# Attention followed by a gated convolution on one core: the order in which one queue issues stores and loads

## The chip, the core and the metric

The kernel runs on one core of a Trainium2 chip. A core has a matrix engine (TensorE, PE in the profile; its weight loads stand apart as PEld), a vector engine (VectorE, DVE), an engine for activation functions and copies (ScalarE, ACT), a general engine (GpSimd, POOL) and a sync engine (SyncE, SP) that computes nothing and here issues every DMA. The engines run at the same time. Each works off its own list of instructions in order and waits at an instruction until what it needs is there. The metric is the time of one execution in microseconds (us) on the device; lower is better.

## What is computed

Two steps, batch 4, 768 positions, 8 heads of 64. First an attention in which each query sees the keys nearer than 16 positions and, beside them, 24 summaries of the whole sequence, one for each block of 32 positions (the maximum of its keys, the mean of its values). Then a gated causal convolution over the 512 joined channels, and an output matrix.

```python
k_sum = k.reshape(B, H, nb, block, D).max(axis=3)          # block 32, nb 24
v_sum = v.reshape(B, H, nb, block, D).mean(axis=3)
scores_l = where(abs(i - j) < 16, scale * q @ k.T, -1e9)
scores_s = scale * q @ k_sum.T + log(block)
a = softmax(concat([scores_l, scores_s]))
x = a @ concat([v, v_sum])                                 # (4, 768, 512)
gate_pre = sum(conv_w[t] * shifted(x, t) for t in range(5))
out = (sigmoid(gate_pre) * (x @ w_val)) @ w_out            # (4, 768, 512) f32
```

## The kernel before

The rows are cut into 12 groups g (batch b and third of the sequence, 256 rows each), and the attention of a group into two units u = 2g and 2g + 1 (four heads each), 24 units in all. A group's result is two tiles `out` of 128 rows by 512 columns, named (g, 0) and (g, 1).

Nothing schedules this program at run time or compile time. One string, `ORDER`, holds some 1,400 tokens such as `S.13.0`; a loop at the end of the kernel function calls for each token the function of that name with those numbers. Each function emits its instructions, so the string sets for every engine the order of its list. A framework adds the waits that the data need. The tokens that matter here:

- `q.g` (line 270), `k.b.pr`, `v.g.e` (line 285), `n.b.pr` (the transposed values `vT`, line 281): loads from HBM, all on SP. `q` has two buffers, `qbd0` and `qbd1`; group g uses number g mod 2.
- `f.g.e` (line 368): an SP copy of the block means into the v tile of group g, inside SBUF. Part e = 0 or 1 serves the even or the odd query tiles of 64 rows.
- `S.u.r` (line 438), PE: scores. `N` (454), DVE: mask and row minimum. `E` (468), ACT: exponentials. `M` (481), POOL: division by the row sum. `T` (490), PE: transposes into `pt`. `C` (494), ACT: copies `pt` to `pts`, which frees the memory for a later `S`. `X` (508), PE: times v.
- `tr.b.pr` (326), POOL (a few DVE): block sums from `vT`.
- `V` (558), `O` (587), PE: the products with `w_val` and `w_out`. `oe.g.si` (597), ACT: evicts an out tile into the SBUF tile `ob`, halved on the way. `st.g.si` (606), SP: stores it.

`op_X` goes through its query tiles in the order 0, 2, 1, 3, so its first half reads part e = 0 of the v tile and its second half part e = 1. The tile `ob` has two buffers for the 24 out tiles; an eviction waits until the store of the tile two before it has left its buffer:

```python
ob = wt(("ob", g, si), [P, DM], "ob")            # a pool with bufs=2
nc.scalar.activation(ob, po, AF.Copy, scale=0.5) # op_oe
...
nc.sync.dma_start(out[b, r0 : r0 + P, w], ob[:, w])  # op_st
```

SP too is in order: a store that waits for its eviction holds every load behind it.

Of the kernel before, what the change touches and what calls it, by code (L numbers as in the profile page):

```python
# [81 lines left out]
G.6 S.12.0 N.12.1 N.12.0 tr.2.1 H.8 I.8.1 N.13.2 N.12.3 N.13.0 E.12.3 k.3.1 f.5.0 N.12.2 N.13.1
M.11.1 A.8.0 A.8.1 A.8.2 O.2.0 oe.2.0 X.9 E.13.0 F.9 I.9.0 st.2.0 v.6.0 E.12.2 I.9.1 A.8.3 A.8.4 H.9
E.12.0 T.10 C.10.0 E.12.1 A.9.0 A.9.1 C.10.1 M.11.0 E.13.1 E.13.2 V.3.0 gf.3.0 A.8.5 A.8.6 A.9.2
A.8.7 V.3.1 gf.3.1 VS.2 vs.2 A.9.3 R.13 A.9.4 A.9.5 R.12 A.9.6 A.9.7 T.11 C.11.0 L.8 L.9 C.11.1 X.10
X.11 gh.3.0 S.14.1 S.15.1 S.15.0 S.14.0 N.14.3 N.14.2 F.10 N.15.1 H.10 h.5 gl.3.0 M.13.0 G.8 H.11
V.4.1 G.9 I.10.1 F.11 I.10.0 I.11.0 I.11.1 gh.3.1 N.14.0 L.10 A.10.0 E.14.3 N.14.1 k.3.3 ks.3.3
# [3 lines left out]
gh.4.0 O.3.0 C.12.0 E.15.0 C.13.0 C.13.1 oe.3.0 M.14.0 gl.4.1 L.11 gl.4.0 S.16.1 f.6.1 S.17.1 S.16.0
S.17.0 E.15.3 G.11 E.15.1 G.10 f.6.0 n.3.0 v.7.0 st.3.1 X.13 I.13.0 ks.3.0 F.13 I.13.1 X.12 N.17.1
V.5.0 H.13 H.12 I.12.1 F.12 kc.3.0 N.16.2 R.15 N.16.3 N.17.0 A.13.0 N.16.0 A.13.1 I.12.0 V.5.1
M.14.1 v.8.0 v.7.1 f.7.1 v.8.1 A.12.0 N.17.2 st.3.0 f.8.0 f.7.0 L.13 E.17.0 gf.5.0 N.17.3 A.12.1
# [9 lines left out]
I.16.1 F.16 gf.7.1 H.16 A.16.0 X.17 S.21.1 I.17.1 gh.7.1 F.17 S.21.0 A.16.1 N.21.1 N.21.0 S.20.1
L.16 M.19.0 I.17.0 S.20.0 A.17.0 E.21.0 H.17 A.17.1 N.20.2 N.21.3 N.20.1 N.21.2 N.20.0 V.7.0 gf.7.0
N.20.3 st.5.0 v.9.0 v.9.1 M.18.0 E.21.3 O.6.1 st.5.1 E.20.2 E.20.0 A.16.2 A.16.3 A.17.2 A.17.3
A.16.4 oe.6.1 VS.3 vs.3 f.9.0 gh.7.0 gl.7.1 A.17.4 A.17.5 A.16.5 A.16.6 T.18 A.17.6 A.17.7 C.18.1
M.19.1 T.19 C.19.1 E.20.3 C.19.0 C.18.0 L.17 V.8.0 E.21.1 G.17 E.21.2 E.20.1 A.16.7 R.20 O.6.0
oe.6.0 f.9.1 X.19 q.11 v.10.1 G.16 H.19 F.19 X.18 I.19.0 v.11.0 S.23.1 h.9 R.21 M.21.1 M.21.0 F.18
# [8 lines left out]
C.22.1 A.20.2 A.20.3 A.20.4 C.22.0 V.10.1 gf.10.1 A.20.5 A.20.6 O.8.0 oe.8.0 A.20.7 G.20 X.22 F.22
X.23 I.22.0 h.11 A.22.0 H.22 L.22 A.22.1 I.22.1 V.10.0 gf.10.0 F.23 H.23 L.23 O.9.1 I.23.0 I.23.1
V.11.0 oe.9.1 A.22.2 st.9.1 A.23.0 A.23.1 gh.10.0 A.23.2 A.23.3 A.23.4 A.23.5 A.23.6 A.23.7 gh.10.1  # L120
gl.10.0 G.23 V.11.1 gf.11.1 A.22.3 st.8.0 O.9.0 oe.9.0 st.9.0 A.22.4 A.22.5 gl.10.1 O.10.1 A.22.6
A.22.7 G.22 gf.11.0 gh.11.0 gh.11.1 O.10.0 gl.11.1 oe.10.1 oe.10.0 st.10.0 gl.11.0 O.11.0 oe.11.0
st.10.1 O.11.1 oe.11.1 st.11.0 st.11.1
"""


# [572 lines left out]
```

## Time and profile before

| | us |
|---|---|
| median of 3 runs | 232.5 (232.01 to 234.11) |
| the profiled execution | 233.51 |
| its span (first to last instruction) | 231.4 |
| PE busy | 218.8 (95% of the span) |
| ACT busy | 187.1 (81%) |
| DVE busy | 171.0 (74%) |
| POOL busy | 150.9 (65%) |
| SP's DMA queue, share of 16 DMA engines | 57.1% |

The profile is of one execution. Busy time is the time in which an engine runs an instruction; issuing a DMA and waiting do not count. On a timeline, a bracket at the end of a row says how long the engine was idle before it, and what ended that. Rows of SP are the times at which it issues a DMA, not those at which the data move. One row can stand for several instructions in a row (x4), and lines are those of the listing above.

### The profile page before, as it was taken

The numbers are of one execution on the slowest core, as the hardware profiler recorded it, in microseconds if no ns is written. First come the engines' busy times: TensorE is split into PE (matmuls) and PEld (weight loads), VectorE is DVE, ScalarE is ACT, GpSimd is POOL, SyncE is SP. The second block draws the span as 40 slices with busy tenths as digits, with TensorE's granted clock in tenths as the row PEclk, the third lists the DMA queues.
The fourth block names the chain that finished last, engine by engine and source line by source line (L and its number), as shares of the span: only waits on it lengthen the run. The fifth ranks groups of instructions, "written<-read, shape, count | busy, mean of one in ns | idle before, by whom it ended". The sixth has DMA issues, their size and how long they took to land.

```text
span 231.4 us, 7645 instructions
## 1 busy us (share of the span) xinstructions
PE 218.8 (95%) x2828; PEld 185.3 (80%) x2828; DVE 171.0 (74%) x699; ACT 187.1 (81%) x614; POOL 150.9 (65%) x207
## 2 busy tenths in 40 slices
...
GB/s 235 341 389 369 408 410 281 406 364 179 318 353 217 283 174 219 305 82 290 284 29 184 183 118 140 180 177 3 130 145 319 89 48 19 46 0 93 45 91 91
DMA packets 17052, 46.50 MB, mean 201 GB/s; under 512 B 2136, under 2 KB 3160, under 8 KB 17016
## 3 DMA queue, kind: packets, MB, share of 16 engines
q1 hardware_dynamic: 17016, 46.02, 57.1%
...
## 4 chain that ended last, share of the span: by engine, by line
PE 66%; DMA 18%; ACT 10%; DVE 4%; issue 1%; SPq 1%; ACTq 0%
PE out L587 23%; PE val L558 23%; DMA k<-in_kT_dram 7%; PE s L438 7%; PE x L508 7%; DMA raw_wo<-in_wo_dram 5%; ACT p L468 4%; PE pt L490 4%; DMA out_dram<-ob 3%; DMA qbd<-in_qT_dram 3%; DVE g L538 2%; PE pw L332 1%; PE vb L342 1%; ACT g L533 1%; DVE sn L454 1%
## 5 line engine op out<-in xcount | busy, mean ns | idle before, releaser
L538 DVE SCALAR_TENSOR_TENSOR g<-xf,cwt,g 128x256 f32<-128x256 f32 x192 | 87.5, 484 | 14.3 <-ACT g L533 8.6
L468 ACT ACTIVATE p<-sn,nm 128x120 f32<-128x120 f32 x192 | 74.0, 396 | 10.5 <-DVE nm L454 10.3
L481 POOL TENSOR_TENSOR p<-p,ri 128x480 f32<-128x480 f32 x48 | 46.8, 991 | 23.9 <-DVE ri L476 21.5
L558 PE MATMUL val<-xh,wv 128*128 128x256 f32 x352 | 49.6, 283 | 0.0
L454 DVE CUSTOM_DVE_ANT_0 sn<-s,mask 128x120 f32<-128x120 f32 x192 | 42.7, 276 | 6.0 <-PE s L438 4.5
L558 PEld LDWEIGHTS val<-xh,wv 128*128 128x128 f32 x352 | 44.5, 188 | 1.4 <-issue 0.3
L587 PE MATMUL out<-wo,gh 128*128 128x512 f32 x176 | 45.1, 398 | 0.0
L572 POOL TENSOR_TENSOR gl<-gf,gh 128x512 fp32r<-128x512 f32 x22 | 28.3, 1294 | 18.1 <-ACT gh L567 18.0
L468 ACT ACTIVATION_READ_ACCUMULATOR p<-sn,nm 128x1 f32 x192 | 38.3, 200 | 0.0
L587 PEld LDWEIGHTS out<-wo,gh 128*128 128x128 f32 x176 | 31.7, 188 | 6.9 <-ACT gt L544 0.2
L524 POOL TENSOR_TENSOR xl<-xf,xh 128x512 fp32r<-128x512 f32 x22 | 28.2, 1292 | 7.9 <-ACT xh L516 7.8
L438 PE MATMUL s<-k,qbd 64*64 64x120 f32 x768 | 26.3, 280 | 6.9 <-POOL k L315 2.7
L438 PEld LDWEIGHTS s<-k,qbd 64*64 64x64 f32 x768 | 21.0, 139 | 11.1 <-POOL k L315 3.9
L326 POOL TENSOR_TENSOR vT<-vT 128x384 f32<-128x384 f32 (+3 forms) x48 | 27.3, 570 | 2.8
L597 ACT ACTIVATE ob<-out 128x512 f32<-128x512 f32 x23 | 13.7, 597 | 18.1 <-PE out L587 14.5
L558 PE MATMUL val<-xl,wv 128*128 128x256 f32 x176 | 27.7, 279 | 0.0
L494 ACT COPY pts<-pt 120x512 f32<-120x512 f32 x48 | 26.3, 589 | 1.5 <-PE pt L490 1.4
L508 PEld LDWEIGHTS x<-pts,v 120*64 120x64 f32 x768 | 23.6, 138 | 3.7 <-ACT pts L494 1.1
L508 PE MATMUL x<-pts,v 120*64 120x64 f32 x768 | 25.4, 224 | 0.4 <-DVE low_wo L394 0.4
L563 DVE SCALAR_TENSOR_TENSOR gf<-gt,val 128x512 f32<-128x512 f32 x24 | 16.4, 685 | 11.9 <-PE val L558 5.7
L587 PE MATMUL out<-wo,gl 128*128 128x512 f32 x88 | 24.1, 395 | 0.0
L558 PEld LDWEIGHTS val<-xl,wv 128*128 128x128 f32 x176 | 23.7, 188 | 0.0
...
## 6 DMA issues: line engine op xcount, KB each, us to landing
...
```

What stands on the lines that cost most here:

```text
L326: nc.gpsimd.tensor_tensor(dst, src[:, :, :n], src[:, :, n : 2 * n], ALU.add)
L438: nc.tensor.matmul(sp[64 * e : 64 * e + 64, h, c * KW : c * KW + KW], qbd[g % NQB][64 * h : 64 * h + 64, pr, i * QT : i * QT + QT], ktile( ...
L454: nc.vector.tensor_tensor_reduce(sn[:, n, :], tiles["s", u][:, h, c * KW : c * KW + KW], mask[:, mv, :], -1.0 / math.sqrt(D), 3.0e38, ALU.add,
L468: nc.scalar.activation(p[:, n, :], tiles["sn", u][:, n, :], AF.Exp, bias=tiles["nm", u][:, n : n + 1], scale=-1.0, accum_out=rs[:, u % NRS ...
L481: nc.gpsimd.tensor_tensor(p[:, w], p[:, w], ri[:, w].unsqueeze(2).broadcast_to([P, TPU, KW]), ALU.mult)
L494: nc.scalar.copy(pts[:, :, QT * e : QT * e + QT], tiles["pt", u][:KW, e])
L508: nc.tensor.matmul(dst, w, src, start=True, stop=True)
L524: nc.gpsimd.tensor_tensor(xl[:, prs(u), :], xf(g)[:, prs(u), HALO:], tiles["xh", g][:, prs(u), :].bitcast(F32), ALU.subtract,)
L538: nc.vector.scalar_tensor_tensor(gt, xf(u // NHP)[:, pr, o : o + SG], cwt[:, pr, o : o + 1], gt, ALU.mult, ALU.add)
L558: nc.tensor.matmul(val[:, r], w, x, start=(n == 0), stop=(n == len(terms) - 1))
L572: nc.gpsimd.tensor_tensor(gl[:, cos, :], tiles["gf", g, cp], tiles["gh", g][:, cos, :].bitcast(F32), ALU.subtract)
L587: nc.tensor.matmul(po, x, w, start=(n == 0), stop=(n == len(terms) - 1))
```

## The change

Only the string `ORDER` changes: 13 of the 24 stores come earlier in SP's list, ahead of loads, copies or another store. The tokens of the loads and of all computing keep their order among themselves. Two pieces of the diff:

```diff
-E.7.2 woc.2 F.4 H.4 A.3.5 R.7 k.2.1 q.5 v.3.0 A.3.6 A.3.7 N.9.3 I.4.0 A.4.0 N.9.2 G.3 gf.1.1 F.5
+E.7.2 woc.2 F.4 H.4 A.3.5 R.7 st.0.0 k.2.1 q.5 v.3.0 A.3.6 A.3.7 N.9.3 I.4.0 A.4.0 N.9.2 G.3 gf.1.1
...
+kc.2.1 F.7 ks.2.0 N.11.0 X.6 I.7.1 H.7 M.9.0 st.1.1 q.7 M.9.1 I.7.0 gl.2.0 A.7.0 N.11.2 A.7.1 A.7.2
...
-n.2.3 A.7.4 v.5.1 v.5.0 st.1.1 A.6.0 A.6.1 A.7.5 H.6 A.7.6 E.11.2 E.11.3 oe.1.0 st.1.0 gl.2.1 h.4
```

The instructions on PE, DVE, ACT and POOL stand in the same order before and after. SP's list changes. In the names below the digits behind the first word are those of the token (`v_4` is the v tile of group 4, `ob_1_1` the evicted tile (1,1)), and the last number only counts. SP's list before, from the copy `f.4.0` on:

```order
L368 DMA v_4_1239<-vs_1_1186 24x2x512
L270 DMA qbd1_70<-in_qT_dram 128x1024
L270 DMA qbd0_69<-in_qT_dram 128x1024
L368 DMA v_4_1239<-vs_1_1186 24x2x512
L281 DMA vT_2_2_1440<-in_vT_dram 128x768
L281 DMA vT_2_3_1449<-in_vT_dram 128x768
L285 DMA v_5_1452<-in_vw_dram 128x1024 x2
L606 DMA out_0_dram<-ob_1_1_1372 128x512
L606 DMA out_0_dram<-ob_1_0_1465 128x512
L368 DMA v_5_1452<-vs_1_1186 24x2x512
L606 DMA out_0_dram<-ob_2_1_1541 128x512
```

and in the same place after the change:

```order
L368 DMA v_4_1240<-vs_1_1187 24x2x512
L606 DMA out_0_dram<-ob_1_1_1372 128x512
L270 DMA qbd1_70<-in_qT_dram 128x1024
L270 DMA qbd0_69<-in_qT_dram 128x1024
L368 DMA v_4_1240<-vs_1_1187 24x2x512
L281 DMA vT_2_2_1441<-in_vT_dram 128x768
L281 DMA vT_2_3_1450<-in_vT_dram 128x768
L285 DMA v_5_1453<-in_vw_dram 128x1024 x2
L606 DMA out_0_dram<-ob_1_0_1465 128x512
L606 DMA out_0_dram<-ob_2_1_1541 128x512
L368 DMA v_5_1453<-vs_1_1187 24x2x512
```

The store of tile (1,1) stood behind the two halves of the v load of group 5. Now it stands ahead of both q loads (groups 7 and 6), of the copy `f.4.1`, of two vT loads and of the v loads. The store of tile (2,1) moves ahead of a copy for group 5.

The second place is on SP, around the stores of group 3. Before:

```order
L273 DMA k_3_2_2050<-in_kT_dram 128x968
L368 DMA v_6_1695<-vs_2_1797 24x2x512 x2
L281 DMA vT_3_0_2177<-in_vT_dram 128x768
L285 DMA v_7_2179<-in_vw_dram 128x1024
L606 DMA out_0_dram<-ob_3_1_2035 128x512
L285 DMA v_8_2301<-in_vw_dram 128x1024
L285 DMA v_7_2179<-in_vw_dram 128x1024
L368 DMA v_7_2179<-vs_2_1797 24x2x512
L285 DMA v_8_2301<-in_vw_dram 128x1024
L606 DMA out_0_dram<-ob_3_0_2127 128x512
```

and after:

```order
L273 DMA k_3_2_2050<-in_kT_dram 128x968
L606 DMA out_0_dram<-ob_3_1_2035 128x512
L368 DMA v_6_1695<-vs_2_1797 24x2x512 x2
L281 DMA vT_3_0_2178<-in_vT_dram 128x768
L606 DMA out_0_dram<-ob_3_0_2127 128x512
L285 DMA v_7_2181<-in_vw_dram 128x1024
L285 DMA v_8_2302<-in_vw_dram 128x1024
L285 DMA v_7_2181<-in_vw_dram 128x1024
L368 DMA v_7_2181<-vs_2_1797 24x2x512
L285 DMA v_8_2302<-in_vw_dram 128x1024
```

The store of (3,1) now stands ahead of the two copies `f.6.1` and `f.6.0`, the load of `vT_3_0` and the first v load of group 7; the store of (3,0), the last of the rows before, is now ahead of the v loads of groups 7 and 8. Of the other moves, `st.0.0` goes ahead of a k load, `q.5` and two v loads; `st.4.0` and `st.5.0` each ahead of a vT load, `st.5.1` ahead of the v loads of group 9, `st.6.1` ahead of the copies and the q load behind them, `st.6.0` ahead of the v loads of groups 10 and 11, `st.7.1` and `st.7.0` each ahead of one load or copy, and `st.10.1` ahead of `st.10.0`.

## Rows read from the trace of the kernel before

**Rows 1.** Busy time, calls and rates by stretch: us, engines, PE clock, DMA share, GB/s.
```profile
0.00:52.00 52.00, 44.34 (x573) 31.01 (x577) 41.22 (x195) 43.23 (x157) 31.55 (x58) 1.00 0.97 356
52.00:86.00 34.00, 33.73 (x520) 29.40 (x517) 32.83 (x131) 32.28 (x113) 31.48 (x46) 1.00 0.77 259
86.00:228.00 142.00, 140.69 (x1740) 124.92 (x1740) 96.56 (x374) 111.40 (x347) 87.89 (x104) 1.00 0.40 133
```

**Rows 2.** Timeline of PE (start us, us, engine, line, operation, tiles; idle in brackets).
```profile
84.01 1.15 PE L508 MATMUL x<-pts,v 120*64 120x64 f32 x32
85.09 0.64 PE L438 MATMUL s<-k,qbd 64*64 64x120 f32 x16
87.05 1.46 PE L438 MATMUL s<-k,qbd 64*64 64x120 f32 x48 [1.32 <-ACT pts L494]
```

**Rows 3.** Timeline of ACT around the eviction that waits.
```profile
75.62 0.57 ACT L597 ACTIVATE ob<-out 128x512 f32<-128x512 f32 x1
...
82.88 1.55 ACT L494 COPY pts<-pt 120x512 f32<-120x512 f32 x3
85.93 0.60 ACT L597 ACTIVATE ob<-out 128x512 f32<-128x512 f32 x1 [1.50 <-DMA out_dram<-ob]
86.42 0.58 ACT L494 COPY pts<-pt 120x512 f32<-120x512 f32 x1
```

**Rows 4.** Chain of waits: start us, us, what.
```profile
28.57 11.05 DMA raw_wo<-in_wo_dram
...
77.90 7.94 DMA out_dram<-ob
```

**Rows 5.** Timeline of SP, its DMA issues from 67 to 83 us.
```profile
67.69 2.79 SPq L368 DMA_DIRECT2D v<-vs  x3
71.42 0.81 SPq L270 DMA_DIRECT2D qbd<-in_qT_dram  x2
72.29 0.82 SPq L368 DMA_DIRECT2D v<-vs  x1
73.15 2.67 SPq L281 DMA_DIRECT2D vT<-in_vT_dram  x2
77.00 0.81 SPq L285 DMA_DIRECT2D v<-in_vw_dram  x2
77.90 0.38 SPq L606 DMA_DIRECT2D out_dram<-ob  x1
```

**Rows 6.** The stretch 72.0 to 75.6 us, columns as in the first group.
```profile
72.00:75.60 3.60, 3.60 (x36) 2.81 (x38) 3.46 (x14) 3.60 (x14) 3.29 (x7) 1.00 0.89 312
```

**Rows 7.** Timeline of SP and PE, 108 to 164 us.
```profile
108.94 1.65 SPq L368 DMA_DIRECT2D v<-vs  x2
...
113.17 0.34 SPq L606 DMA_DIRECT2D out_dram<-ob  x1
...
118.29 2.08 PE L508 MATMUL x<-pts,v 120*64 120x64 f32 x64
...
163.13 1.70 SPq L368 DMA_DIRECT2D v<-vs  x2
```

**Rows 8.** The stretch 163.1 to 166.1 us, columns as in the first group.
```profile
163.10:166.10 3.00, 3.00 (x38) 2.93 (x34) 2.89 (x7) 3.00 (x10) 0.00 (x0) 1.00 0.32 69
```

**Rows 9.** Timeline of POOL and PE, 83 to 100 us.
```profile
83.04 2.51 POOL L326 TENSOR_TENSOR vT<-vT 128x384 f32<-128x384 f32 x4
...
94.79 1.94 POOL L481 TENSOR_TENSOR p<-p,ri 128x480 f32<-128x480 f32 x2
...
99.42 0.69 PE L490 MATMUL pt<-ident,p 64*120 64x64 f32 x16
```

**Rows 10.** Timeline of SP, ACT and PE, 55 to 63 us.
```profile
55.08 0.51 SPq L273 DMA_DIRECT2D k<-in_kT_dram  x1
57.26 0.33 SPq L270 DMA_DIRECT2D qbd<-in_qT_dram  x1
...
55.64 0.58 ACT L597 ACTIVATE ob<-out 128x512 f32<-128x512 f32 x1
...
62.56 1.05 PE L438 MATMUL s<-k,qbd 64*64 64x120 f32 x32
```

More of the change, by code (lines that the diff above doesn't have):

```diff
@@ L70 @@
 M.6.0 E.7.0 N.7.2 N.7.3 S.9.1 G.2 gf.1.0 A.3.4 N.9.0 f.2.0 f.2.1 X.5 X.4 V.1.1 E.7.1 E.7.3 N.9.1
-E.7.2 woc.2 F.4 H.4 A.3.5 R.7 k.2.1 q.5 v.3.0 A.3.6 A.3.7 N.9.3 I.4.0 A.4.0 N.9.2 G.3 gf.1.1 F.5
-tr.1.0 S.10.1 H.5 S.10.0 N.10.1 gh.1.0 A.4.1 L.4 gh.1.1 I.5.0 I.4.1 N.10.2 N.10.3 E.10.3 I.5.1
+E.7.2 woc.2 F.4 H.4 A.3.5 R.7 st.0.0 k.2.1 q.5 v.3.0 A.3.6 A.3.7 N.9.3 I.4.0 A.4.0 N.9.2 G.3 gf.1.1
+F.5 tr.1.0 S.10.1 H.5 S.10.0 N.10.1 gh.1.0 A.4.1 L.4 gh.1.1 I.5.0 I.4.1 N.10.2 N.10.3 E.10.3 I.5.1
 N.10.0 ks.2.1 A.4.2 A.5.0 L.5 gl.1.0 A.4.3 M.7.0 M.8.0 T.6 gl.1.1 M.7.1 A.5.1 A.4.4 A.4.5 A.5.2
@@ L74 @@
 A.4.6 A.4.7 VS.1 vs.1 V.2.0 V.2.1 A.5.3 v.4.1 S.11.0 E.9.0 E.9.2 E.10.0 C.6.0 E.10.2 C.6.1 G.4 A.5.4
-gf.2.0 E.9.3 E.10.1 gh.2.0 st.0.0 v.3.1 ks.2.2 R.10 A.5.5 A.5.6 k.2.0 v.4.0 A.5.7 S.11.1 N.11.3
-E.9.1 R.9 h.3 T.7 wob.1 wob.2 C.7.0 n.2.0 tr.2.0 O.1.1 C.7.1 f.3.1 f.3.0 X.7 f.4.0 G.5 gf.2.1 oe.1.1
-N.11.1 kc.2.1 F.7 ks.2.0 N.11.0 X.6 I.7.1 H.7 M.9.0 q.7 M.9.1 I.7.0 gl.2.0 A.7.0 N.11.2 A.7.1 A.7.2
+gf.2.0 E.9.3 E.10.1 gh.2.0 v.3.1 ks.2.2 R.10 A.5.5 A.5.6 k.2.0 v.4.0 A.5.7 S.11.1 N.11.3 E.9.1 R.9
@@ L78 @@
+h.3 T.7 wob.1 wob.2 C.7.0 n.2.0 tr.2.0 O.1.1 C.7.1 f.3.1 f.3.0 X.7 f.4.0 G.5 gf.2.1 oe.1.1 N.11.1
+kc.2.1 F.7 ks.2.0 N.11.0 X.6 I.7.1 H.7 M.9.0 st.1.1 q.7 M.9.1 I.7.0 gl.2.0 A.7.0 N.11.2 A.7.1 A.7.2
 O.1.0 I.6.0 q.6 F.6 E.11.0 I.6.1 gh.2.1 kc.2.2 M.8.1 f.4.1 n.2.2 ks.2.3 kc.2.0 M.10.1 kc.2.3 A.7.3
-n.2.3 A.7.4 v.5.1 v.5.0 st.1.1 A.6.0 A.6.1 A.7.5 H.6 A.7.6 E.11.2 E.11.3 oe.1.0 st.1.0 gl.2.1 h.4
-tr.2.2 A.6.2 A.6.3 M.10.0 L.6 T.9 T.8 C.8.1 L.7 C.8.0 tr.2.3 C.9.1 O.2.1 oe.2.1 C.9.0 E.11.1 A.7.7
-G.7 X.8 F.8 A.6.4 S.13.0 f.5.1 S.12.1 A.6.5 A.6.6 R.11 st.2.1 n.2.1 I.8.0 S.13.1 N.13.3 E.13.3 A.6.7
@@ L82 @@
[L82 to L87, printed above, removed]
@@ L88 @@
-A.11.0 gf.4.1 gl.3.1 V.4.0 N.15.3 gh.4.1 E.14.0 E.14.2 A.10.1 O.3.1 q.8 E.14.1 N.15.2 E.15.2 n.3.3
-q.9 oe.3.1 M.12.0 v.6.1 k.3.0 N.15.0 A.11.1 A.10.2 A.10.3 A.11.2 gf.4.0 A.11.3 k.3.2 A.10.4 A.11.4
+n.2.3 A.7.4 v.5.1 v.5.0 A.6.0 A.6.1 A.7.5 H.6 A.7.6 E.11.2 E.11.3 oe.1.0 st.1.0 gl.2.1 h.4 tr.2.2
+A.6.2 A.6.3 M.10.0 L.6 T.9 T.8 C.8.1 L.7 C.8.0 tr.2.3 C.9.1 O.2.1 oe.2.1 C.9.0 E.11.1 A.7.7 G.7 X.8
+F.8 A.6.4 S.13.0 st.2.1 f.5.1 S.12.1 A.6.5 A.6.6 R.11 n.2.1 I.8.0 S.13.1 N.13.3 E.13.3 A.6.7 G.6
+S.12.0 N.12.1 N.12.0 tr.2.1 H.8 I.8.1 N.13.2 N.12.3 N.13.0 E.12.3 k.3.1 f.5.0 N.12.2 N.13.1 M.11.1
@@ new lines @@
+A.8.0 A.8.1 A.8.2 O.2.0 oe.2.0 X.9 E.13.0 F.9 I.9.0 st.2.0 v.6.0 E.12.2 I.9.1 A.8.3 A.8.4 H.9 E.12.0
+T.10 C.10.0 E.12.1 A.9.0 A.9.1 C.10.1 M.11.0 E.13.1 E.13.2 V.3.0 gf.3.0 A.8.5 A.8.6 A.9.2 A.8.7
+V.3.1 gf.3.1 VS.2 vs.2 A.9.3 R.13 A.9.4 A.9.5 R.12 A.9.6 A.9.7 T.11 C.11.0 L.8 L.9 C.11.1 X.10 X.11
+gh.3.0 S.14.1 S.15.1 S.15.0 S.14.0 N.14.3 N.14.2 F.10 N.15.1 H.10 h.5 gl.3.0 M.13.0 G.8 H.11 V.4.1
+G.9 I.10.1 F.11 I.10.0 I.11.0 I.11.1 gh.3.1 N.14.0 L.10 A.10.0 E.14.3 N.14.1 k.3.3 ks.3.3 A.11.0
+gf.4.1 gl.3.1 V.4.0 N.15.3 gh.4.1 E.14.0 E.14.2 A.10.1 O.3.1 q.8 E.14.1 N.15.2 E.15.2 n.3.3 q.9
@@ L90 @@
+oe.3.1 M.12.0 v.6.1 k.3.0 N.15.0 A.11.1 A.10.2 A.10.3 A.11.2 gf.4.0 A.11.3 k.3.2 A.10.4 A.11.4
 A.11.5 A.11.6 R.14 h.6 M.12.1 kc.3.3 M.13.1 ks.3.2 T.12 C.12.1 A.11.7 T.13 A.10.5 A.10.6 A.10.7
[L91 to L94, printed above, removed]
+gh.4.0 O.3.0 C.12.0 E.15.0 C.13.0 C.13.1 oe.3.0 M.14.0 gl.4.1 L.11 gl.4.0 S.16.1 st.3.1 f.6.1 S.17.1
@@ L95 @@
+S.16.0 S.17.0 E.15.3 G.11 E.15.1 G.10 f.6.0 n.3.0 st.3.0 v.7.0 X.13 I.13.0 ks.3.0 F.13 I.13.1 X.12
+N.17.1 V.5.0 H.13 H.12 I.12.1 F.12 kc.3.0 N.16.2 R.15 N.16.3 N.17.0 A.13.0 N.16.0 A.13.1 I.12.0
+V.5.1 M.14.1 v.8.0 v.7.1 f.7.1 v.8.1 A.12.0 N.17.2 f.8.0 f.7.0 L.13 E.17.0 gf.5.0 N.17.3 A.12.1
 A.12.2 N.16.1 E.16.3 E.16.2 E.16.0 E.16.1 gh.5.0 M.15.0 L.12 M.15.1 A.12.3 A.13.2 A.13.3 A.13.4
@@ L99 @@
 S.18.0 I.14.1 S.18.1 N.18.2 R.16 M.16.1 N.18.3 E.18.3 H.14 O.4.0 oe.4.0 A.14.0 A.15.0 N.19.3 N.19.2
-L.14 E.19.3 L.15 A.15.1 A.15.2 M.16.0 N.19.1 A.14.1 A.14.2 n.3.2 A.14.3 V.6.0 gf.6.0 N.18.0 st.4.0
+L.14 E.19.3 L.15 A.15.1 A.15.2 M.16.0 N.19.1 A.14.1 A.14.2 st.4.0 n.3.2 A.14.3 V.6.0 gf.6.0 N.18.0
 f.8.1 q.10 E.19.0 N.18.1 gh.6.1 E.19.2 M.17.0 M.17.1 A.14.4 A.15.3 A.14.5 A.15.4 A.14.6 A.15.5
-A.15.6 E.18.1 E.18.2 gh.6.0 E.18.0 R.18 O.5.0 oe.5.0 A.14.7 gl.6.0 tr.3.2 M.18.1 n.3.1 tr.3.1 gl.6.1
-V.7.1 T.16 C.16.0 E.19.1 T.17 C.17.0 A.15.7 C.17.1 G.14 C.16.1 G.15 O.5.1 oe.5.1 R.19 X.16 I.16.0
@@ L104 @@
[L104 to L109, printed above, removed]
@@ L110 @@
-H.18 I.19.1 gf.8.0 M.20.0 v.10.0 A.19.0 S.22.1 I.18.0 A.18.0 I.18.1 S.22.0 A.18.1 S.23.0 st.6.1
+A.15.6 E.18.1 E.18.2 gh.6.0 E.18.0 R.18 O.5.0 oe.5.0 A.14.7 gl.6.0 tr.3.2 M.18.1 st.5.0 n.3.1 tr.3.1
+gl.6.1 V.7.1 T.16 C.16.0 E.19.1 T.17 C.17.0 A.15.7 C.17.1 G.14 C.16.1 G.15 O.5.1 oe.5.1 R.19 X.16
+I.16.0 I.16.1 F.16 gf.7.1 H.16 A.16.0 X.17 S.21.1 I.17.1 gh.7.1 F.17 S.21.0 A.16.1 N.21.1 N.21.0
+S.20.1 L.16 M.19.0 I.17.0 S.20.0 A.17.0 E.21.0 H.17 A.17.1 N.20.2 N.21.3 N.20.1 N.21.2 N.20.0 V.7.0
+gf.7.0 N.20.3 st.5.1 v.9.0 v.9.1 M.18.0 E.21.3 O.6.1 E.20.2 E.20.0 A.16.2 A.16.3 A.17.2 A.17.3
@@ L111 @@
+A.16.4 oe.6.1 VS.3 vs.3 st.6.1 f.9.0 gh.7.0 gl.7.1 A.17.4 A.17.5 A.16.5 A.16.6 T.18 A.17.6 A.17.7
+C.18.1 M.19.1 T.19 C.19.1 E.20.3 C.19.0 C.18.0 L.17 V.8.0 E.21.1 G.17 E.21.2 E.20.1 A.16.7 R.20
+O.6.0 oe.6.0 f.9.1 X.19 q.11 st.6.0 v.10.1 G.16 H.19 F.19 X.18 I.19.0 v.11.0 S.23.1 h.9 R.21 M.21.1
+M.21.0 F.18 H.18 I.19.1 gf.8.0 M.20.0 v.10.0 A.19.0 S.22.1 I.18.0 A.18.0 I.18.1 S.22.0 A.18.1 S.23.0
 M.20.1 h.10 N.23.0 N.22.0 N.23.2 A.19.1 gl.7.0 L.18 N.22.1 E.22.0 V.8.1 N.22.2 gf.8.1 f.10.1 L.19
 N.23.1 N.22.3 gh.8.0 gl.8.0 A.19.2 A.18.2 N.23.3 O.7.1 E.22.1 gh.8.1 gl.8.1 V.9.1 E.22.3 E.23.2
-oe.7.1 E.22.2 E.23.0 st.6.0 A.18.3 A.18.4 R.22 M.22.1 A.18.5 A.19.3 A.19.4 A.19.5 O.7.0 oe.7.0
```

19 lines of the change are left out of this document (10 added, 9 removed).

## The prediction

> **What bounds the kernel now.** I read first how busy each engine is in three stretches of the span [rows 1]. From 86 to 228 us TensorE (PE) is busy for 140.69 of 142.00 us, and from 52 to 86 for 33.73 of 34.00: it is the bound, at full granted clock (1.00), and its matmuls run one behind the other in a fixed order. Whatever the change gains, it must gain as idle time of PE behind 52 us, since the first store that moves stands behind that point, and there is little to gain: 1.31 us behind 86 and 0.27 ahead of it. Most of it is one hole: PE's timeline shows the score matmuls of unit 13 begin at 85.09, and the next score matmuls only at 87.05, with 1.32 us idle, put down to ScalarE's copy of a transposed tile (pts) [rows 2].
>
> Next I asked why that copy is late. On ScalarE's timeline three pts copies end at 82.88 + 1.55 = 84.43; then stands the eviction `oe.2.1`, which waits 1.50 us for "DMA out_dram<-ob" and begins at 85.93; the pts copy that PE waits for stands right behind it [rows 3]. The chain of waits names the store: it was issued at 77.90 and landed 7.94 us later, at 85.84 [rows 4]. That store is `st.1.1`: `ob` has two buffers, so the eviction of tile (2,1) reuses the buffer of (1,1). Its data was ready long before: `oe.1.1` ended at 75.62 + 0.57 = 76.19 [rows 3]. SP issued it only at 77.90 because it came behind two v loads at 77.00 [rows 5], and those 2 x 512 KB, with the vT loads ahead of them, were then ahead of the store in the DMA engines. It is the only place behind 52 us where PE pays for a store.
>
> **What the change removes.** No instruction is added or dropped, and the order on PE, ACT, DVE and POOL is the same; only SP's order differs. `st.1.1` now stands ahead of `q.7`, `q.6` and `f.4.1`. SP has nothing left to do at 67.69 + 2.79 = 70.48 [rows 5] and in the new order waits there for `oe.1.1` until 76.19. The store then goes out at 76.2 with no transfer ahead of it. If it took as long as the slowest case of this stretch, 7.94 us [rows 4], it would land at 84.1, still before ScalarE is free at 84.43 [rows 3]. At the 312 GB/s that the transfers of 72.0 to 75.6 us got [rows 6], its 262 KB take 0.8 us of data, so it lands well ahead of that. So the 1.50 us of ScalarE goes, and with it PE's 1.32: the next matmuls follow unit 13's at about 85.73. Gain: 1.32 us. (The Trainium skill, page "DMA: Bandwidth & Descriptors", section "Anatomy of one DMA", prices a transfer at 2.0 us plus its bytes at 436 GB/s, fitted for another issue path; that is 2.6 us for this store and an estimate of 78.8 for its landing. The sum would be the same.)
>
> **What it adds: SP does wait.** The words of the change say that a store moves where SP need not wait; by this trace it waits at three places, and every load behind the store goes out later.
>
> At `st.1.1`, `q.7` goes from 71.42 to about 76.6, `q.6` to 77.0, and the copy `f.4.1` (block means into the v tile of group 4) from 72.29 to about 77.5: 5.2 us later each (issues 0.4 us apart, [rows 5]). Who needs them? `X.8` begins at 84.01 and reads the rows that `f.4.1` writes in its second half, so from about (84.01 + 85.09) / 2 = 84.55; the score matmuls of unit 13 read `q.6` at 85.09 [rows 2]. In the trace, 312 GB/s over 3.6 us are 1.12 MB [rows 6], about what the three transfers hold (2 x 524 KB + 98 KB): their data was through some 4.3 us after the issue of `q.7`. The same 4.3 us from 76.6, plus 0.8 us for the store's data ahead, give 81.7. The other bound is the store that took 7.94 us: 77.5 + 7.94 = 85.4 for `f.4.1`, 84.9 for `q.6`. So PE waits between 0 and 0.9 us; I take 0, because [rows 6] is of the very same transfers and the cover is 2.8 us. (The Trainium skill speaks against the change here: the same page, "Rules for kernel authors", says to issue a DMA early and wait for it late, and these loads lose 5.2 us of their head start. By the rule alone that would be a loss; by the rows it is paid out of cover.)
>
> Behind them the load of `vT_2_2` moves from 73.15 [rows 5] to about 78.3. POOL adds up its halves at 83.04, without having waited [rows 9]. With 393 KB more at 312 GB/s, 1.3 us, it lands at about 81.7 + 1.3 = 83.0, and by the slow bound at 78.3 + 7.94 = 86.2: POOL is 0 to 3.2 us late. POOL has no gap from there to the scaling of unit 11's p, which ends at 94.79 + 1.94 = 96.73; PE needs it for the transposes at 99.42 [rows 9], or 98.10 once PE is 1.32 us earlier. That is a cover of 1.37 us, so the price is between 0 and 1.8 us. I take 0.
>
> At `st.3.1` SP waits for `oe.3.1`, until about 113.14, before the two copies `f.6.1` and `f.6.0`, which went out at 108.94; `X.13` reads them at 118.29 [rows 7]. All of these move with PE, so I leave the 1.32 out: store at 113.2, copies at 113.6 and 114.4. Two such copies alone, issued from 163.13 [rows 7], had moved their 0.2 MB by 166.1 [rows 8], 3.0 us later. So they are there at about 116.6 and the cover is 1.7 us. With 7.94 us from 114.4 they would be 4.0 us late, but only the store is ahead of them. I take 0.
>
> At `st.0.0` SP waits from 55.08 to the end of `oe.0.0`, 55.64 + 0.58 = 56.22; the k load behind it slips by 1.5 us, and `q.5`, which waited for PE until 57.26 in any case, gets 262 KB more ahead of it, 0.8 us of data. The matmuls that read it begin at 62.56, 5.3 us behind its issue [rows 10]. Price 0, by the slow bound 57.26 + 7.94 - 62.56 = 2.6 us. The later moves are alike, in a stretch where the DMA engines are busy for 0.40 of the time and not 0.77 [rows 1]. I take 0 for them too.
>
> **The sum.** The profiled execution took 233.5 us, its span 231.4 of them. 233.5 - 1.32 = 232.2, which is 0.9943 of it. The median of the three runs is 232.5, lower than the profiled execution; the same share of it gives 231.2 us.
>
> **The rivals.**
> 1. A late load takes back part of the gain, or the gap was smaller in the median run than in the profiled one (its 1.0 us excess is nearly the gap itself). For: POOL's cover of 1.37 us and `X.8`'s of 2.8 are both less than the spread between 4.3 and 7.94 us. Against: no single transfer need be that slow. PE then waits 0.3 to 1.3 us, or gains as much less: 231.5 to 232.5, say 232.0.
> 2. Slower than before: `f.4.1` comes so late that `X.8` holds PE for longer than the hole it closes. It decides at 84.55 + 1.32 = 85.87, that is 8.4 us behind its issue. For: in the first 52 us, with transfers at 356 GB/s throughout [rows 1], a load took 11.05 us [rows 4]; from 77.5 that is 88.5, a wait of 4.0 us and 235.2. Two such loads ahead of the copy can hardly do that, but a smaller excess can: 10 us give 87.5, a wait of 2.9 and 234.1. Against: SP stood idle for 5.7 us and the DMA engines begin empty.
> 3. The change does not do what it says: the eviction waits for something else in the store's place. Against: PE has delivered tile (2,1) when `X.8` begins at 84.01, and the buffer is free by 84.1 at the latest. If so: 232.5.
>
> **How the numbers follow.** Full gain, 231.2 (230.3 to 231.8 with the spread of single runs): 0.53. Rival 1: 0.27. Rival 2: 0.12. Rival 3: 0.05. Something faster that I do not see, a gap elsewhere that only the unprofiled runs have: 0.03. To keep 8 in 10 the range runs from 230.2 to 233.6: it takes in the full gain, rivals 1 and 3, and the near half of rival 2. About 1% is what a measurement of this kernel can tell from no change; 1% of 232.5 is 2.3 us, more than all of PE's idle time behind 52 us. Faster by over 1% (below 230.2): 0.06. Slower (above 234.8): 0.08. Within: 0.86.
>
> **What would show it.** Right: PE's timeline has no gap behind unit 13's score matmuls; `oe.2.1` begins at about 84.4 without a wait for a DMA; `st.1.1` goes out at 76.2 and `q.7` behind it at 76.6; PE's busy time from 86 on is as before and its last matmul ends 1.3 us earlier. Wrong: PE idle before `X.8`'s second half or unit 13's scores, put down to a DMA of v or qbd; POOL idle before the vT sums of batch 2 and PE idle at unit 11's transposes; or PE idle before `X.13`, put down to a DMA of v.

## The result, and the profile of the changed kernel

| | before | after |
|---|---|---|
| median of 20 runs each, us | 232.38 (230.74 to 234.11) | 234.57 (232.16 to 237.13) |
| the profiled execution, us | 233.51 | 234.72 |
| its span, us | 231.4 | 232.6 |
| PE idle from 52 to 220 us in it | 1.32 | 2.47 |

The ratio is 1.0071, with a 95% interval of 1.0047 to 1.0094: slower by about 1.7 us. It compares executions of the faster of two states in which they come: two of the changed kernel's, 236.35 and 237.13 us, are left out of it, so it lies below the ratio of the two medians, 1.0094. I had forecast 231.2 us with a range up to 233.6. The change is within 1%, as forecast, but on the other side, and outside the range.

The busy time by stretch, the columns as in [rows 1] (us, busy time and calls of PE, PEld, DVE, ACT and POOL, PE clock, DMA share, GB/s):

```profile
52.00:86.00 34.00, 32.60 (x487) 28.61 (x488) 31.51 (x128) 32.96 (x115) 29.07 (x41) 1.00 0.65 218
86.00:220.00 134.00, 132.93 (x1744) 118.98 (x1740) 97.95 (x378) 108.49 (x342) 87.99 (x107) 1.00 0.44 146
```

PE is idle for 1.40 us in the first stretch, where [rows 1] has 0.27, and for 1.07 in the second; before, 1.32 us in both together was nearly all the one gap of [rows 2]. First the place at which the change aimed, on ACT and on PE:

```profile
77.09 0.57 ACT L597 ACTIVATE ob<-out 128x512 f32<-128x512 f32 x1
...
84.40 1.56 ACT L494 COPY pts<-pt 120x512 f32<-120x512 f32 x3
85.82 0.64 ACT L597 ACTIVATE ob<-out 128x512 f32<-128x512 f32 x1
86.31 0.63 ACT L494 COPY pts<-pt 120x512 f32<-120x512 f32 x1
```

```profile
85.55 1.15 PE L508 MATMUL x<-pts,v 120*64 120x64 f32 x32
86.63 1.87 PE L438 MATMUL s<-k,qbd 64*64 64x120 f32 x64
```

The eviction `oe.2.1` stands right behind the three pts copies, without a bracket, and the 64 score matmuls run as one row: the gap of [rows 2] and the wait of [rows 3] are gone. But PE has two gaps that it did not have:

```profile
64.05 1.05 PE L438 MATMUL s<-k,qbd 64*64 64x120 f32 x32 [1.39 <-DMA qbd<-in_qT_dram]
...
100.55 0.69 PE L490 MATMUL pt<-ident,p 64*120 64x64 f32 x16 [1.07 <-POOL p L481]
```

The first are the score matmuls of unit 10, which stood at 62.56 without a wait [rows 10]; the second are unit 11's transposes, at 99.42 in [rows 9]. SP's issues show what is late:

```profile
56.92 0.35 SPq L606 DMA_DIRECT2D out_dram<-ob  x1
57.32 0.69 SPq L273 DMA_DIRECT2D k<-in_kT_dram  x1
58.12 0.40 SPq L270 DMA_DIRECT2D qbd<-in_qT_dram  x1
...
77.69 0.35 SPq L606 DMA_DIRECT2D out_dram<-ob  x1
78.09 1.92 SPq L270 DMA_DIRECT2D qbd<-in_qT_dram  x2
80.05 0.82 SPq L368 DMA_DIRECT2D v<-vs  x1
80.98 0.92 SPq L281 DMA_DIRECT2D vT<-in_vT_dram  x2
```

Both stores go out right behind their evictions. `k.2.1`, which went out at 55.08 [rows 10], now does so at 57.32, right ahead of `q.5`; the vT load goes out at 80.98 instead of 73.15 [rows 5]. The chain of waits holds both loads:

```profile
58.12 5.79 DMA qbd<-in_qT_dram
...
80.98 5.74 DMA vT<-in_vT_dram
```

And POOL, which in [rows 9] began the vT sums at 83.04 without a wait, waits for that load and then has no gap as far as the scaling of unit 11's p:

```profile
86.80 2.50 POOL L326 TENSOR_TENSOR vT<-vT 128x384 f32<-128x384 f32 x4 [2.24 <-DMA vT<-in_vT_dram]
...
98.56 1.93 POOL L481 TENSOR_TENSOR p<-p,ri 128x480 f32<-128x480 f32 x2
```

In the two profiled executions the sum is plain: -1.32 for the gap that went, +1.39 and +1.07 for the two that came, +1.14 us, and the spans differ by 1.2.

### The profile page after: what moved, and what is told of

Its sections match the earlier page's. It is cut to its first block, busy times and chain, and to the rows that moved or that the text cites. A ratio compares the mean times of both kernels' runs of the same rounds, so it can differ in the third digit from the quotient of the medians.

```text
span 232.6 us, 7645 instructions
## 1 busy us (share of the span) xinstructions
PE 218.3 (94%) x2828; PEld 185.3 (80%) x2828; DVE 171.3 (74%) x699; ACT 187.0 (80%) x614; POOL 151.0 (65%) x207
## 4 chain that ended last, share of the span: by engine, by line
PE 64%; ACT 12%; DMA 11%; POOL 6%; SPq 3%; issue 2%; DVE 0%; POOLq 0%; ACTq 0%
PE out L587 23%; PE val L558 22%; PE x L508 7%; PE s L438 7%; ACT p L468 5%; DMA qbd<-in_qT_dram 5%; DMA v<-in_vw_dram 4%; PE pt L490 4%; POOL vT L326 3%; DMA vT<-in_vT_dram 2%; ACT pts L494 2%; POOL p L481 1%; ACT g L533 1%; POOL xl L524 1%; ACT sc_wo L386 1%
## 5 line engine op out<-in xcount | busy, mean ns | idle before, releaser
L468 ACT ACTIVATION_READ_ACCUMULATOR p<-sn,nm 128x1 f32 x192 | 39.3, 205 | 0.0
```

The costliest lines, as they stand in the source:

```text
L468: nc.scalar.activation(p[:, n, :], tiles["sn", u][:, n, :], AF.Exp, bias=tiles["nm", u][:, n : n + 1], scale=-1.0, accum_out=rs[:, u % NRS ...
```

## The experiments

All of them change SP's list alone, except the third buffer; the order on PE, ACT, DVE and POOL stays that of the kernel before. Each was timed against the kernel before on the same chip, with 6 to 12 runs in the comparison unless it says otherwise; the ratios have intervals of about 0.0022 to 0.0045 to either side. A diff shows pieces of the string `ORDER`.

### The two moves, one at a time

Each of the two new gaps belongs to one move. First `st.0.0` alone:

```diff
-R.7 k.2.1 q.5 v.3.0
+R.7 st.0.0 k.2.1 q.5 v.3.0
...
-gh.2.0 st.0.0 v.3.1
+gh.2.0 v.3.1
```

> The kernel before with one store moved: st.0.0 stands ahead of k.2.1 as in the changed kernel; st.1.1 and all others stay. Theory A (two separate costs in the changed kernel: the load q.5 comes late through st.0.0, and POOL's vT sums come late through st.1.1): PE waits 1.0 to 1.7 us for the q load ahead of unit 10's scores (it was 1.39), none at unit 11's transposes, and the 1.3 us hole for the store stays; 1.0 to 1.5 us slower than before, ratio 1.004 to 1.007. Rival B (the loss of the changed kernel comes from st.1.1 and what follows alone, the wait for q.5 swallows a later wait): the wait is there but the ratio is 0.999 to 1.002.

Measured: 1.0004 (0.9969 to 1.0039), where rival B had it and not theory A. PE waits 1.31 us for `q.5`, and the later gap is gone without having been touched: PE and ACT come to `oe.2.1` later, and the old store has landed. One wait takes the place of the other. Because the ratio is lower than such a wait makes one expect, it was run again:

> The kernel before with st.0.0 alone moved ahead of k.2.1, once more. If PE's wait for q.5 there is in every execution (1.3 us, 0.0056 of the time) and before has the later gap in few of its executions: ratio 1.003 to 1.0055. If the wait comes in some executions only, or is made good later: 0.999 to 1.002, as in the first set (1.0004).

Measured: 1.0012 (0.9986 to 1.0039), again with the wait and without the later gap (timeline of PE, and the chain of waits, in which the load of `q.5` stands):

```profile
63.86 1.05 PE L438 MATMUL s<-k,qbd 64*64 64x120 f32 x32 [1.49 <-DMA qbd<-in_qT_dram]
...
86.39 1.87 PE L438 MATMUL s<-k,qbd 64*64 64x120 f32 x64
```

```profile
57.70 6.02 DMA qbd<-in_qT_dram
```

Then the changed kernel without this move, and the kernel before with `st.1.1` alone:

```diff
-R.7 st.0.0 k.2.1 q.5 v.3.0
+R.7 k.2.1 q.5 v.3.0
...
-gh.2.0 v.3.1
+gh.2.0 st.0.0 v.3.1
```

> The changed kernel with st.0.0 back in its old place, all other stores as changed. Theory A: PE does not wait for the q load at unit 10; it still waits about 1.1 us for POOL at unit 11's transposes, and the hole for the store is gone; within 0.3 us of before, ratio 0.998 to 1.001. Rival B: as slow as the changed kernel, ratio 1.005 to 1.009.

```diff
-M.9.0 q.7 M.9.1
+M.9.0 st.1.1 q.7 M.9.1
...
-v.5.1 v.5.0 st.1.1 A.6.0
+v.5.1 v.5.0 A.6.0
```

> The kernel before with one store moved: st.1.1 ahead of q.7, where the change has it. Theory A (the vT load pushed back is the price of this move): PE's gap of 1.32 us in front of the scores behind unit 13 is closed, POOL waits about 1.3 us for vT_2_2 and PE 0.3 to 1.1 us at unit 11's transposes: ratio 0.9955 to 0.9985. Theory B (the price of this move is larger than one profile shows, since the kernel with only st.0.0 put back gave 1.0024): ratio 1.000 to 1.003. Theory C (this move costs nothing, what costs are the moves further back): no PE gap at unit 11's transposes, ratio 0.994 to 0.9955.

Measured: 1.0024 (0.9997 to 1.0051) and 1.0013 (0.9987 to 1.0038), the first above the range of its theory A, the second in that of theory B. In both, no wait for `q.5` and no gap ahead of unit 12's scores, but the late vT; POOL and PE of the kernel with `st.1.1` alone:

```profile
84.78 2.50 POOL L326 TENSOR_TENSOR vT<-vT 128x384 f32<-128x384 f32 x4 [1.40 <-DMA vT<-in_vT_dram]
```

```profile
98.53 0.69 PE L490 MATMUL pt<-ident,p 64*120 64x64 f32 x16 [0.45 <-POOL p L481]
```

So this move too closes a gap and opens another. Both together, and nothing else:

> The kernel before with two of the thirteen moves alone: st.0.0 ahead of k.2.1 and st.1.1 ahead of q.7. Theory A (they carry the whole loss): PE waits 1.1 to 1.5 us for qbd at unit 10's scores and 0.5 to 1.5 us at unit 11's transposes; ratio 1.004 to 1.0095, the changed kernel's. Rival B (others of the moves cost too): ratio 0.998 to 1.003, with the waits as above or smaller.

Measured: 1.0086 (1.0054 to 1.0118), the whole loss of the change. The profiled execution, 232.63 us, was the fastest of this kernel: it has 0.51 us at unit 11's transposes and no wait for `q.5`, though the order there is that of the change:

```profile
62.65 1.05 PE L438 MATMUL s<-k,qbd 64*64 64x120 f32 x32
```

The wait for `q.5` thus isn't in every execution, and one profile of it would have misled. The changed kernel was run again as well:

> The changed kernel once more, unchanged: a second profiled execution, and its time beside the kernels of this set. If its loss is a part of every execution: ratio 1.004 to 1.0095, PE waits 1.0 to 1.5 us for qbd at unit 10's scores and 0.5 to 1.5 us at unit 11's transposes. If the wait for qbd comes and goes with the transfer, as in the kernel with the two moves alone (no wait in the profile, but 1.0086 over all its executions): the same ratio, with a wait anywhere between 0 and 1.5 us in the profile.

Measured: 1.0073 (1.0034 to 1.0111), with PE waiting 1.44 us for `q.5` and 0.76 at unit 11's transposes.

### Is the gap of the kernel before always there?

Three edits close the gap with no load held back. A buffer of its own for the tile (2,1):

```diff
-ob = wt(("ob", g, si), [P, DM], "ob")
+ob = (once(("ob", 2, 1), lambda: cpool.tile([P, DM], F32, tag="raw", name="ob_2_1")) if (g, si) == (2, 1) else wt(("ob", g, si), [P, DM], "ob"))
```

> The kernel before in its old order; only the eviction of out tile (2,1) writes into a buffer of its own (memory that held a raw weight at the start), so that it waits for no store. Theory A: the eviction begins at about 84.4 us, PE's hole of 1.3 us before unit 12's scores is gone, nothing else changes; ratio 0.994 to 0.996. Rival C (the hole was a matter of the profiled execution, or the next wait stands right behind it): ratio 0.998 to 1.001.

The store `st.1.1` only ahead of the v loads that stood in its way, or also ahead of the vT loads but behind `q.7`, `q.6` and `f.4.1`:

```diff
-n.2.3 A.7.4 v.5.1 v.5.0 st.1.1
+n.2.3 A.7.4 st.1.1 v.5.1 v.5.0
```

> The kernel before with one store moved: st.1.1 stands behind the loads q.7, q.6, f.4.1 and both vT loads and ahead of the two v loads of group 5, which wait for PE until 77.0 us in any case. Theory A: SP waits for the eviction less than 0.5 us, no load goes out later than before by more than 0.3 us, the hole of 1.3 us is gone, and no wait of PE comes in its place; ratio 0.994 to 0.996. Rival C: 0.998 to 1.001.

```diff
-M.8.1 f.4.1 n.2.2 ks.2.3
+M.8.1 f.4.1 st.1.1 n.2.2 ks.2.3
```

> The kernel before with st.1.1 behind q.7, q.6 and f.4.1 and ahead of the vT loads: the q loads go out as before, the vT loads wait for the eviction. Theory A (the price of moving this store is the late vT): q.7, q.6 and f.4.1 go out at 71 to 74 us, POOL waits 0 to 1.5 us for vT_2_2, since three fewer transfers stand ahead of it than in the change, PE waits 0 to 0.5 us at unit 11's transposes: ratio 0.996 to 1.000. Rival B (what costs is that loads wait behind a store at all): ratio 1.001 to 1.004.

Measured: 0.9984 (0.9955 to 1.0014), 0.9966 (0.9936 to 0.9996), 0.9981 (0.9952 to 1.0010). None of the three profiles has the gap or a wait for a load in its place; PE in the second of them:

```profile
84.74 1.87 PE L438 MATMUL s<-k,qbd 64*64 64x120 f32 x64
```

That is a gain of 0.4 to 0.8 us and not 1.32, with intervals that reach from no gain to about 1.5 us; the first ratio lies in the range of its rival C. So the kernel before was profiled twice more:

> The kernel before once more, unchanged, for a second profiled execution. Theory A (PE's gap of 1.32 us in front of the scores behind unit 13 is there in every execution): a gap of 1.0 to 1.6 us there, ended by the eviction that waited for the store st.1.1. Theory C (the gap is an accident of the profiled execution, in which the last part of the store came 3.4 us after its first): the store lands in 4 to 6 us and PE has no gap there, or one under 0.4 us; then there was little to gain for the change.

> The kernel before once more, for a third profiled execution. Theory C (the gap of 1.32 us is an accident of the first profiled execution): no gap of more than 0.4 us in front of the scores behind unit 13, the store st.1.1 lands in 5 to 7 us. If the gap is there in about half the executions, it may be found again, at 0.5 to 1.5 us.

One execution each, without an interval: 231.42 and 233.27 us. The first has no gap (ACT and PE):

```profile
82.44 1.55 ACT L494 COPY pts<-pt 120x512 f32<-120x512 f32 x3
84.12 0.60 ACT L597 ACTIVATE ob<-out 128x512 f32<-128x512 f32 x1
```

```profile
83.59 1.15 PE L508 MATMUL x<-pts,v 120*64 120x64 f32 x32
84.67 2.04 PE L438 MATMUL s<-k,qbd 64*64 64x120 f32 x64
```

the second has it, with the store in the chain of waits and on PE:

```profile
78.22 7.66 DMA out_dram<-ob
```

```profile
87.09 1.46 PE L438 MATMUL s<-k,qbd 64*64 64x120 f32 x48 [1.01 <-ACT pts L494]
```

So the gap is 1.32, 0 and 1.01 us in three executions, 0.78 on average. It comes and goes with one transfer. It is not all that differs: in the first 52 us, which no move touches, PE is idle for 7.66 us in the first execution and for 6.53 in the second. In the two executions that have the gap the store is late while the DMA engines are half idle: the first profile before it lands, then the third (columns as in [rows 1]):

```profile
83.00:84.50 1.50, 1.50 (x21) 1.04 (x21) 1.43 (x5) 1.43 (x3) 1.42 (x3) 1.00 0.53 205
84.50:85.90 1.40, 1.23 (x40) 0.93 (x34) 1.33 (x5) 0.00 (x0) 1.17 (x5) 1.00 0.36 94
```

```profile
83.00:85.90 2.90, 2.90 (x55) 2.25 (x53) 2.79 (x8) 1.77 (x4) 2.66 (x6) 1.00 0.47 158
```

With about half of the 16 engines' time unused on average, their total data rate does not explain when the store lands. Whether a single engine was behind the others, these averages don't show, and what holds the store's last part stays open.

### What makes `q.5` late

The prediction counted the store's 262 KB as what comes ahead of `q.5`. But the store, waiting at the head of SP's list for its eviction, also holds the k load of 484 KB back until just ahead of `q.5`. The order tells the two apart:

```diff
-R.7 k.2.1 q.5 v.3.0
+R.7 st.0.0 q.5 k.2.1 v.3.0
...
-gh.2.0 st.0.0 v.3.1
+gh.2.0 v.3.1
```

> The kernel before with st.0.0 ahead and the load k.2.1 behind q.5, so SP's order is st.0.0, q.5, k.2.1. Theory A (the 484 KB of the k load, held back by the store until just ahead of q.5, are what makes q.5 late): q.5 lands 3.6 to 4.4 us behind its issue, PE does not wait at unit 10's scores, ratio 0.997 to 1.001. Rival B (the store's 262 KB ahead of q.5 are enough): q.5 takes 5 us or more, PE waits 0.5 to 1.4 us there, ratio 1.000 to 1.004.

Measured: 0.9983 (0.9959 to 1.0006), and no wait (SP, then PE):

```profile
56.73 0.35 SPq L606 DMA_DIRECT2D out_dram<-ob  x1
57.18 0.65 SPq L270 DMA_DIRECT2D qbd<-in_qT_dram  x1
57.88 0.45 SPq L273 DMA_DIRECT2D k<-in_kT_dram  x1
```

```profile
62.36 1.05 PE L438 MATMUL s<-k,qbd 64*64 64x120 f32 x32
```

The store is still ahead of `q.5`, and the load is there within 62.36 - 57.18 = 5.18 us, where it took 5.79 to 6.02 in the four profiles with the wait. Its issue came 0.5 us earlier too (57.18 for 57.68 and 57.70 with `st.0.0` alone), but that is less than the waits of 1.31 and 1.49 us that went: most of it is the k load. In two more kernels below with `q.5` ahead of the k load PE does not wait for `q.5` either. The Trainium skill, page "DMA: Bandwidth & Descriptors", section "Queues, rings and completion order", says that on each DMA engine the descriptors are consumed in the order of their ring; the trace agrees, 484 KB put ahead turned no wait into 1.31 to 1.49 us in four of five profiles. The profile of this kernel has no gap ahead of unit 12's scores, though `st.1.1` stands in its old place. In the changed kernel, the store behind both loads, and then one more load of 512 KB ahead of `q.5`:

```diff
-R.7 st.0.0 k.2.1 q.5 v.3.0
+R.7 k.2.1 q.5 st.0.0 v.3.0
```

> The changed kernel with st.0.0 behind q.5, and so also behind k.2.1, and still ahead of the v loads; all else as changed. Theory A (the store's data ahead of the q load are what makes PE wait at unit 10's scores): no wait for qbd there, q.5 lands 3.5 to 4.5 us behind its issue, POOL still waits 1 to 2 us for vT; ratio 0.999 to 1.004, like the changed kernel with st.0.0 back in its old place (1.0024). Rival B (the early store costs by its share of the DMA engines, wherever it stands): ratio 1.004 to 1.009.

```diff
-R.7 st.0.0 k.2.1 q.5 v.3.0
+R.7 st.0.0 k.2.1 v.3.0 q.5
```

> The changed kernel with one more load, v.3.0 with 512 KB, put ahead of q.5. Theory A (what stands ahead of q.5 in the DMA engines sets PE's wait at unit 10's scores): at about 390 GB/s the 512 KB add 1.3 us to the wait, so 2.4 to 3.0 us in the profile, and the ratio goes from 1.007 to about 1.013 (1.009 to 1.016). Rival B (the wait there is given back further on, or is not what costs): the ratio stays at 1.005 to 1.009.

Measured: 1.0013 (0.9984 to 1.0041), without a wait for `q.5` (which doesn't tell store and k load apart, since neither is held back ahead of it); and 1.0152 (1.0108 to 1.0197), with this on PE:

```profile
65.32 1.05 PE L438 MATMUL s<-k,qbd 64*64 64x120 f32 x32 [2.66 <-DMA qbd<-in_qT_dram]
```

The 512 KB added 1.27 us to the wait of 1.39, as expected from the data rate. The ratio rose by 0.0081 or 1.9 us; the last section goes into the rest.

### Which of the loads behind `st.1.1` cost

Here the vT loads stand ahead of the store, the q loads and the copy behind it:

```diff
-M.9.0 q.7 M.9.1
+M.9.0 n.2.2 n.2.3 st.1.1 q.7 M.9.1
```

> The kernel before with st.1.1 ahead of q.7, and with the two loads of vT_2_2 and vT_2_3 put ahead of that store. Theory A (the late vT is the price): POOL's block sums of batch 2 begin without a wait for a DMA and PE has no gap at unit 11's transposes; q.7, q.6 and f.4.1 go out at 76.6 to 78 us as in the change and are there when X.8's second half and unit 13's scores need them: ratio 0.994 to 0.9975, the whole gain of the closed gap. Rival B (the price is the q loads and the copy behind the store): PE still waits for a DMA at X.8 or at unit 13's scores, ratio 0.998 to 1.003. If PE has the gap at unit 11's transposes all the same, A is wrong.

Measured: 1.0007 (0.9980 to 1.0034), as rival B had it. The wait for vT is gone, as expected, but PE waits at the place of my second rival, in the middle of `X.8`:

```profile
85.64 0.69 PE L508 MATMUL x<-pts,v 120*64 120x64 f32 x16 [0.66 <-DMA v<-vs]
```

So moving only the vT loads out of the store's way isn't enough; the copy `f.4.1` has little cover too. In the kernel that kept the q loads and the copy ahead of the store (0.9981) the vT loads stand behind it, go out from 76.08 us, and POOL does not wait for them. So what cost was not the store alone but the q loads and the copy held back with the vT loads; it is the store that has to go further back.

### The changed kernel, mended

Three kernels keep the other eleven moves:

```diff
-R.7 st.0.0 k.2.1 q.5 v.3.0
+R.7 k.2.1 q.5 v.3.0
...
-gh.2.0 v.3.1
+gh.2.0 st.0.0 v.3.1
...
-M.9.0 st.1.1 q.7 M.9.1
+M.9.0 q.7 M.9.1
...
-n.2.3 A.7.4 v.5.1 v.5.0
+n.2.3 A.7.4 st.1.1 v.5.1 v.5.0
```

> The changed kernel with two stores put elsewhere: st.0.0 back ahead of v.3.1, where it was before, and st.1.1 behind the vT loads and ahead of the v loads of group 5. The other eleven moves stay. Theory A (those two moves alone carry the loss): no PE wait for qbd at unit 10's scores, no POOL wait for vT, no gap in front of the scores behind unit 13; ratio 0.994 to 0.9985, like the kernel before with only the second of these edits (0.9966). Rival B (the eleven others cost some tenths of a per cent in the executions that are not profiled): ratio 0.999 to 1.003.

```diff
-R.7 st.0.0 k.2.1 q.5 v.3.0
+R.7 st.0.0 q.5 k.2.1 v.3.0
```

> The changed kernel with the load k.2.1 behind q.5; st.0.0 stays ahead of both, all else as changed. Theory A (the k load held back by the store makes q.5 late; what is left of the loss then is the late vT alone): no wait for qbd at unit 10's scores, PE 0.4 to 1.1 us idle at unit 11's transposes; ratio 0.999 to 1.004, against 1.007 of the change. Rival B (the eleven other moves or the late vT carry the loss): ratio 1.005 to 1.009.

```diff
-R.7 st.0.0 k.2.1 q.5 v.3.0
+R.7 st.0.0 q.5 k.2.1 v.3.0
...
-M.9.0 st.1.1 q.7 M.9.1
+M.9.0 q.7 M.9.1
...
-n.2.3 A.7.4 v.5.1 v.5.0
+n.2.3 A.7.4 st.1.1 v.5.1 v.5.0
```

> The changed kernel with k.2.1 behind q.5 and st.1.1 between the vT loads and the v loads of group 5. All thirteen stores still stand earlier than in the kernel before. Theory A: no wait for qbd, none for vT and none for the store; ratio 0.996 to 0.9995, of the size that the gap of the kernel before is worth on average (0.9966, 0.9984 and 1.0004 where it was closed without a new wait). Rival B (moving stores early has a price of its own): ratio 1.001 to 1.004.

Measured: 1.0004 (0.9982 to 1.0027), 1.0037 (1.0010 to 1.0063) and 0.9972 (0.9944 to 0.9999). The first lies in rival B's range (the eleven others cost something), though its profile has no wait behind 53 us; the third is where it was expected. In the second, POOL waits 1.10 us for vT in the profile and PE for nothing, against the 0.4 to 1.1 us expected; but that execution, 232.25 us, was the fastest of its twelve.

**What the ratios say together.** Five kernels move the store `st.1.1`, or give its tile a buffer, with nothing late in the gap's place by their profiles: 0.9984, 0.9966, 0.9981, 1.0004, 0.9972, on average 0.9981. Four have vT late and no wait for `q.5`: 1.0013, 1.0024, 1.0013, 1.0037, on average 1.0022. Three have both moves as the change has them: 1.0071, 1.0073, 1.0086, on average 1.0077. So by these averages the gap is worth 0.0019 or 0.4 us, the late vT costs 0.0041 or 1.0 us, and the late `q.5` 0.0055 or 1.3 us; for the late loads this is about the largest that the profiles show for each, and more than they show on average. Two things don't fit. `st.0.0` alone should by this sum be at 0.9981 + 0.0055 = 1.0036 and was at 1.0004 and 1.0012; both intervals end at 1.0039, so it may be noise, and if it is not, what gives about 0.6 us back stays open. And the kernel with `st.0.0` ahead of `q.5` and the k load behind, which leaves `st.1.1` where it was, is at 0.9983: whether the 0.4 us are the gap's alone is not shown.

## Why the prediction was wrong, by its own steps

- **The gain.** The mechanism was right: the store lands early, the eviction does not wait, PE's gap is gone. The size was not. I took 1.32 us from one execution; two more show 0 and 1.01, and the kernels that close the gap without a load late in its place are faster by 0.4 us on average. My first rival named this doubt (the excess of the profiled execution over the median) and I gave it too little weight.
- **The step at `st.0.0`, price 0.** This failed: PE waits 1.39 us, within the slow bound of 2.6. I put the store's 262 KB ahead of `q.5` and wrote of the k load only that it slips by 1.5 us. It slips to a place right ahead of `q.5`, and it has 484 KB. Before, it had gone out 2.2 us ahead of `q.5` [rows 10]. Moved behind `q.5`, it costs nothing that shows (0.9983).
- **The step at `st.1.1`, vT.** This failed as well: POOL was late by 2.24 us, within the bounds of 0 to 3.2, and PE by 1.07, within 0 to 1.8; I took 0 for both. I had the load go out at 78.3 and land at 83.0. It went out at 80.98 and took 5.74 us. Of the 2.7 us, the eviction's end gives 1.47 (77.09 + 0.57 = 77.66 for 76.19; half of that the whole program was late already at `st.0.0`, 56.92 for 56.22, the rest is about half of PE's wait for `q.5`), and the two issues of `q.7` and `q.6` took 1.92 for 0.81 (0.92 in the second profile of the change). The price 0 rested on transfers that ran at 312 GB/s [rows 6], which I took for the q loads and the copy alone; the vT loads went out from 73.15 on [rows 5], so part of those 1.12 MB may be theirs. With two terms each somewhere between 0 and some 2 us, the middle of the bounds would have been nearer than their lower end.
- **The two steps are not independent.** I summed gains and prices place by place. A wait upstream moves PE past the later gap (`st.0.0` alone: gap gone, no gain). So two moves that each come out near zero (1.0004 and 1.0012; 1.0013) cost 0.7 to 0.9% together: the gap can be saved only once.
- **Right:** `X.8` and unit 13's scores have no wait in the change, nor has `X.13` behind the copies of group 6, which go out at 114.79 where 113.6 was forecast; the eleven other moves cost nothing that can be told from noise (with them 1.0071 and 1.0073, 1.0024, 1.0004; without them, otherwise alike, 1.0086, 1.0013, 0.9966; the last pair lies at the edge of what its intervals allow). The rule that I weighed, of the Trainium skill, page "DMA: Bandwidth & Descriptors", section "Rules for kernel authors", to issue a DMA early and wait for it late, spoke against the change. For vT the trace agrees: it went out at 80.98 instead of 73.15 and came late; `q.5` itself went out only 0.86 us later (58.12 for 57.26), and the k load ahead of it did the rest.
- **The rivals.** Rival 1 had the place of the second loss, with 0.3 to 1.3 us, but only as a part of the gain given back. Rival 2, the slower one, named `X.8`, which did not wait in the change and did when vT was put ahead (0.66 us).
